# One block-maximum task of each B unit moves from the last group of a slot into the first group of the next slot

## The chip, the cores and the metric

The kernel runs on one core of one Trainium2 chip. The metric is the device time of one execution in microseconds. Engines are called as in the profile: PE is the matrix engine, PEld its weight loads, DVE the vector engine, ACT the scalar engine, POOL the GpSimd engine, SP the queue that issues most DMAs.

## The reference, cut to what matters

Two attentions over the same 2048 tokens (width 512, 32 heads of 16) are mixed by a gate. A is a segmented attention with a compressive memory: four segments of 512 tokens, each with softmax inside the segment. B is an ordinary attention over all 2048 keys:

```
qkv = (x @ wqkv)...;  scores = q k^T * Dh**-0.5;  p = softmax(scores);  o = p v      # B
out = g * (A @ wo_a) + (1 - g) * (B @ wo_b)
```

The softmax needs the maximum of each row of scores before the exponentials. Here that maximum comes from a separate product: the scores are computed twice, once only for their maxima, once transposed for the exponentials.

## The kernel before, in words

After a projection phase (about the first 335 us) the work is 32 units of A and 32 of B; a unit is four heads by 512 queries. They are done in 32 **slots**, loop variable `k`: slot `k` does B unit `32 + k` and then A unit `k`. A slot has 37 **groups**, loop variable `n`: groups 0 to 31 are B's, groups 32 to 36 are A's. The order in which each engine takes instructions is the order in which this code writes them.

A B group is written by `t_group` and `pvs`. `t_group` (line 537) issues two matmuls of 64 rows by 128 keys by 512 queries, here called T0 (rows 0 to 63 of the array) and T1 (rows 64 to 127), into two of the three score banks `tb`, `tb`, `mb`, and ACT takes the exponential of each (line 543). `pvs` issues the product of earlier exponentials with V into the one bank `pvb` (line 559).

Beside its own work, slot `k` computes the maxima of units that come later. The list `plan[k, n]` holds these tasks. A **B task** `s_b` (lines 474 and 476) is two matmuls S (rows 64 to 127, then rows 0 to 63) into one of two buffers `sbk` (two banks each, taken in turn by `rot("s", SBK)`) and one DVE reduction over both banks. Each B unit has 32 of them. For `k >= 1` the tasks of unit `33 + k` are spread one to a group, twelve over groups 20 to 31 of slot `k - 1` and twenty over groups 0 to 19 of slot `k`. In slot 0 some of groups 0 to 19 have two tasks. Six **A tasks** `s_a` (lines 452 to 462) with their reductions follow the T matmuls of A groups 32 to 36.

A B task stands between T0 and T1 of its group (argument `between`), so that S on rows 64 to 127 runs beside T0, and S on rows 0 to 63 beside T1.

At group 0 `pvs` finishes the previous A unit: the last product into `pvb`, then `fin_copy` (line 566), a DVE copy of `pvb` to `pvs`. Group 1 has no V product. From slot 9 on, group 1 is followed by `out_mm` (line 625), twelve matmuls of the output projection. Group 2 starts the next use of `pvb`.

Of the kernel before, what the change touches and what calls it, by code (L numbers as in the profile page):

```python
# [23 lines left out]
NT = SEQ // 128  # L24
# [10 lines left out]
def gated_mix_kernel(ctx, tc, xt, wq, wk, wv, wo, beta, wqkv, wob, gate_w, out):  # L35
# [370 lines left out]
    def load_q(u):  # L406
        kd, qd, c = UN[u]
        load_qk(q_of(u), kd, 0, qd, c)

    def load_ka(u):  # L410
        kd, qd, c = UN[u]
        load_qk(KA[u % 2], kd, 1, qd, c)

    def load_kb(k, c=None):
        dst = KB[k % 3] if c is None else KB[k % 3][:, :, c * C:(c + 1) * C]
        load_qk(dst, "B", 1, k % 8, c)
# [6 lines left out]
    def load_vb(g):  # L423
        v_src(VB[g % 2], "B", g % 4, None)

    def load_va(u):
        kd, qd, c = UN[u]
        v_src(VA[(u // 2) % 2], "A", qd // 2, c)
# [51 lines left out]
    def m_chain(k):  # L480
        mx = pair_max(k)
        if k == 1:
            nc.vector.memset(mx[:, 0], 0.0)
        if k < 32:
            nc.vector.tensor_reduce(mx[:, 1], MXB.pop(32 + k).rearrange("q j p i c -> q (j p) i c"), axis=AX.X,
                                    op=OP.max)
        else:
            nc.vector.memset(mx[:, 1], 0.0)
        del MX[k]
        mx = mx.rearrange("q u h i -> q (u h i)")  # L490
        m8 = M8[k] = W.tile([128, 2, 32], FT, name="m8")
        hi = W.tile([128, 32], FR, name="mhi")
        if 8 <= k < 32:
            nc.gpsimd.tensor_scalar(mx, mx, -1.0, None, op0=OP.mult)
            nc.gpsimd.tensor_copy(hi, mx)
            nc.gpsimd.tensor_copy(m8[:, 0], hi)
            nc.gpsimd.tensor_tensor(m8[:, 1], mx, hi, op=OP.subtract)
        else:
            nc.vector.tensor_scalar(hi, mx, -1.0, None, op0=OP.mult)
            nc.vector.tensor_copy(m8[:, 0], hi)  # L500
            nc.vector.scalar_tensor_tensor(m8[:, 1], mx, -1.0, hi, op0=OP.mult, op1=OP.subtract)
# [20 lines left out]
    def t_group(u, n, banks, between=()):  # L522


        kd, qd, c = UN[u]
        bs = [bank(banks) for _ in range(2)]
        c0 = 0
        for it, hs in (((n // 2, (n % 2 * 2, n % 2 * 2 + 1)),) if kd == "B" else GA[n]):
            q0 = 128 * it if kd == "A" else 0
            w = C - q0  # L530
            pn = it if kd == "B" else it % 2
            for j, h in enumerate(hs):
                if j:
                    for f in between:
                        f()
                r = slice(64 * j, 64 * j + 64)
                nc.tensor.matmul(bs[j][:, c0:c0 + w], k_of(u, h // 2)[r, 128 * it:128 * it + 128],  # L537
                                 q_of(u)[r, h // 2, q0:], start=True, stop=True)
                PT[u, it, h] = PTILE[pn % 2][:, 2 + j if (kd, it) == ("A", 2) else h][:, c0:c0 + w]
            c0 += w  # L540
        for j in range(2):
            pt = PTILE[pn % 2][:, 2 + j if (kd, n) == ("A", 4) else hs[j]]
            nc.scalar.activation(pt, bs[j], AF.Exp, scale=SCALE)  # L543
            if kd == "A":
                m = pt[:, :128] if n < 2 else pt.rearrange("p (a t) -> p a t", a=4)[:, ::3 if n < 4 else 2]
                nc.gpsimd.affine_select(out=m, in_=m, pattern=[[1, 128]] if n < 2 else [[0, 2], [1, 128]],  # L546
                                        compare_op=OP.is_ge, fill=0.0, base=0, channel_multiplier=-1)
# [119 lines left out]
    def todo(fn, *a):  # L667
        return lambda: fn(*a)
# [90 lines left out]
    for blk in range(16):  # L759
# [9 lines left out]
        n = blk + 1 + (c == 2)  # L769
# [74 lines left out]
    def late():  # L844
        proj.close()
        L = AT["L"] = ctx.enter_context(tc.tile_pool(name="late", bufs=1))
        VB[1] = L.tile([128, NT, 8, E + 1], FT, name="vb1")
        AT["o"] = [L.tile([128, 4, 2, C], FT, name=f"o{n}") for n in range(2)]
        AT["wh"] = L.tile([128, 4, 2, DM], FR, name="wh")
        AT["wl"] = L.tile([128, 4, 2, DM], FR, name="wl")  # L850
        AT["d"] = [L.tile([128, C], FT, name=f"d{n}") for n in range(2)]
        AT["oh"] = L.tile([128, 4, 2, 128], FR, name="oh")
        AT["ol"] = L.tile([128, 4, 2, 128], FR, name="ol")
        for p in range(2):
            set_aux(KB[2][:, p], 0)
# [6 lines left out]
    def pvs(k, n):  # L862

        ua, ub = k, 32 + k
        if n == 0:
            if k:
                pv(ua - 1, 2)
                fin_copy(ua - 1)
        elif k == 31 and n < 2 * NT:
            if n % 2 and n > 1:  # L870
                pv(ub, n // 2 - 1)
        elif 2 <= n < 2 * NT + 2:
            pv(ub, n // 2 - 1, n % 2 * 256, n % 2 * 256 + 256)
            if n == 2 * NT + 1:
                fin_copy(ub)
        elif n > 2 * NT + 1:
            m = n - 2 * NT - 2
            if m < 2:
                pv(ua, 0, 256 * m, 256 * m + 256)
            else:  # L880
                pv(ua, 1)
                pv(ua, 3)
# [13 lines left out]
    def beside(k, it):  # L896

        for f, it0, u in ((fin_load, NT + 1, 32 + k), (fin_rec, 5, 31 + k), (fin_bc, 6, 31 + k),
                          (fin_load, 1, k - 1), (fin_rec, 6, k - 1), (fin_bc, S_LAST + 2, k - 1)):
            if it == it0 and (k or it0 > NT):  # L900
                f(u)
        c, j = divmod(k - 1, 8)
        if k and j % 2:
            for kd, it0 in (("B", 9), ("A", 13)):
                if it == it0:
                    fin_norm(kd, j // 2, c)
        if k >= 8 and k % 2 == 0 and it == NT + 2:
            out_split(k // 8 - 1, k // 2 % 4)
        if (k, it) == (31, 4):
            grest = AT["grest"] = AT["o"][0][64:, 0, 0]  # L910
            nc.sync.dma_start(grest, GD[3 * C:].rearrange("(o t) -> o t", o=1).to_broadcast([64, C]))
        if (k, it) == (31, 9):
            grest = AT["grest"]
            nc.vector.tensor_scalar(grest, grest, nh[64:, 3:4], None, op0=OP.mult)
        if (k, it) == (31, NT + 2):
            fin_rec(63)
        if k == 31 and it == 13:
            o = AT["o"][1][:64, 3, 0]
            nc.gpsimd.tensor_tensor(o, o, AT["d"][0][:64], op=OP.mult)
        if k == 31 and it < 8 and it % 2 == 0:  # L920
            for a in range(2):
                tail_split(it // 2, slice(0, 3), a)
# [3 lines left out]
    plan = {}  # L926
# [5 lines left out]
    for k in range(31):  # L932
# [5 lines left out]
        for n, t in enumerate(ST_A):  # L938
            plan.setdefault((k, 2 * NT + n - (n > 2)), []).append(todo(s_a, k + 1, *t))

    for k in range(32):
        ua, ub = k, 32 + k
        banks = T3 + [b[:, 0] for b in SBK] * (k == 31)
        for n in range(NG):
            it = n // 2 if n < NG - 1 else NT + 2
            mid = plan.pop((k, n)) if n < 2 * NT and (k, n) in plan else []
            t_group(*(ub, n) if n < 2 * NT else (ua, n - 2 * NT), banks, mid)
            for f in plan.get((k, n), []) + ex[k][0].get(n, []):
                f()
            pvs(k, n)  # L950
            for f in ex[k][1].get(n, []):
                f()
            if n % 2 == 0 and n < NG - 1:
                continue
            beside(k, it)
            if it == S_LAST:
                m_chain(k + 1)
            if it == 4 and not k:
                late()
            if it == 4 and not k:  # L960
                load_q(ub + 2)
                for c in range(NC4):
                    load_kb(2, c)
            if it == NT and k < 29:
                load_q(ub + 3)
                load_kb(k + 3)
            if it == 6 and k < 31:
                load_q(ua + 1)
                load_ka(ua + 1)
                if (ua + 1) % 2 == 0:  # L970
                    load_va(ua + 1)
            if it == 9:
                if k % 2 == 0 and k < 30:
                    load_vb(k // 2 + 1)
                if 1 <= k <= 4:
                    load_wo(k - 1)
# [55 lines left out]
```

## Time and profile before

| what | value |
|---|---|
| time, median of 3 runs | 1946.82 us (1943.4 to 2188.65) |
| profiled execution, its own time | 1946.74 us |
| its span, first to last instruction | 1945.0 us |
| mean granted PE clock | 0.997 |
| busy share of the span | PE 99%, DVE 83%, ACT 74%, POOL 15% |

The span is what the trace covers; the profiled execution's own time is 1.74 us more and lies 0.08 us from the median. A row of the timeline has the start, the length, the engine, the line, the operation with its output and inputs, and in square brackets the idle time of that engine just before with what ended it. Rows that follow each other with the same form are merged (x2, x8).

### The profile page before, as it was taken

To read this page: it belongs to the slowest core of one execution; us is meant where nothing else is said; L and a number is where in the kernel's file an instruction comes from. 1 tells how busy PE (TensorE), PEld (TensorE's weight loads), DVE (VectorE), ACT (ScalarE), POOL (GpSimd) and SP (SyncE) were. 2 spreads that over 40 slices of the span, in tenths; PEclk is the share of its full clock that TensorE was granted. 3 is DMA by queue.
4 is the path that set the end of the run, shared out by engine and by line. 5 is a ranking of instruction groups with operands and counts; after the bars stand their busy time and mean duration, and the time that the engine had idled before them with its cause. 6 is when DMAs were issued, how large, how long until landed. Compare 5 with 4: busy or idle time off the path is not lost.

```text
span 1945.0 us, 43560 instructions
## 1 busy us (share of the span) xinstructions
PE 1922.5 (99%) x17485; PEld 931.0 (48%) x17485; DVE 1622.1 (83%) x1726; ACT 1434.8 (74%) x2699; POOL 298.4 (15%) x593
## 2 busy tenths in 40 slices
PE   7999999999999999999999999999999999999999
PEld 5887777444344444444444444444444444444445
DVE  6135766899999999999999999999999999999942
ACT  4233333688888888888888888888888888888884
POOL 5200000011111111111111111111111111111022
PEclk9999999999999999999999999999999999999999
DMA  7666656745444444443445454544444443434111
GB/s 217 163 207 185 196 193 173 176 96 116 98 117 88 105 87 105 87 116 87 116 87 114 87 115 87 116 88 108 94 97 107 96 105 87 104 87 110 50 48 58
DMA packets 163790, 222.49 MB, mean 114 GB/s; under 512 B 39916, under 2 KB 90556, under 8 KB 157828
## 3 DMA queue, kind: packets, MB, share of 16 engines
q1 hardware_dynamic: 159284, 211.41, 44.1%
q0 software_dynamic: 3248, 8.03, 2.3%
q8 instruction: 138, 2.26, 0.5%
q14 instruction: 64, 0.52, 0.1%
q10 hardware_dynamic: 1056, 0.26, 0.1%
HBM read 147.95 MB, written 68.16 MB: 111 GB/s over the span
## 4 chain that ended last, share of the span: by engine, by line
PE 96%; DVE 2%; DMA 1%; SPq 1%; issue 0%; ACT 0%; DVEq 0%; ACTq 0%
PE pvb L559 33%; PE tb L537 18%; PE sbk L474 12%; PE mb L537 9%; PE tb L304 5%; PE sbk L452 3%; PE tb L625 2%; PE mb L304 2%; PE sbk L287 1%; PE tb L287 1%; PE mb L625 1%; PE pvb L304 1%; PE sbk L456 1%; PE mb L287 1%; PE pvb L287 1%; PE tb L652 1%
## 5 line engine op out<-in xcount | busy, mean ns | idle before, releaser
L476 DVE TENSOR_REDUCE mxb<-sbk 128x2 f32<-128x1024 f32 x1024 | 1225.8, 1223 | 61.0 <-PE tb L537 30.6
L543 ACT ACTIVATE raw<-tb 128x512 f32<-128x512 f32 x1555 | 887.6, 598 | 148.2 <-PE tb L537 103.6
L559 PE MATMUL pvb<-raw,vb 128*17 128x256 f32 (+1 forms) x8072 | 639.9, 388 | 0.0
L543 ACT ACTIVATE raw<-mb 128x512 f32<-128x512 f32 x782 | 467.6, 598 | 72.3 <-PE mb L537 45.7
L474 PE MATMUL sbk<-xh,qb 64*128 64x512 f32 x1344 | 477.6, 444 | 3.5 <-DVE mxb L476 2.1
L537 PE MATMUL tb<-qb,xh 64*128 64x512 f32 x872 | 353.3, 443 | 0.0
L559 PEld LDWEIGHTS pvb<-raw,vb 128*17 128x17 f32 x8072 | 135.0, 95 | 341.3 <-issue 335.9
L474 PE MATMUL sbk<-kb,qb 64*128 64x512 f32 x704 | 240.9, 444 | 0.0
L537 PEld LDWEIGHTS tb<-qb,xh 64*128 64x128 f32 x872 | 146.4, 184 | 176.6 <-issue 90.1
L537 PE MATMUL mb<-qb,xh 64*128 64x512 f32 x445 | 199.0, 447 | 0.0
L474 PEld LDWEIGHTS sbk<-xh,qb 64*128 64x128 f32 x1344 | 190.6, 184 | 8.7 <-DVE mxb L476 6.3
L537 PE MATMUL tb<-qb,kb 64*128 64x512 f32 x470 | 191.0, 446 | 0.9 <-DVE st L314 0.9
L546 POOL TENSOR_SCALAR_AFFINE_SELECT raw<-raw 128x256 f32<-128x256 f32 (+1 forms) x320 | 115.6, 361 | 357.7 <-ACT raw L543 349.9
L460 DVE TENSOR_REDUCE mx<-sbk 128x2 f32<-128x768 f32 (+1 forms) x128 | 136.7, 1090 | 23.7 <-PE sbk L456 20.9
L537 PEld LDWEIGHTS mb<-qb,xh 64*128 64x128 f32 x445 | 82.0, 184 | 94.9 <-issue 50.6
L537 PEld LDWEIGHTS tb<-qb,kb 64*128 64x128 f32 x470 | 79.2, 184 | 99.0 <-issue 53.1
L599 POOL TENSOR_TENSOR o<-o,d 128x512 f32<-128x512 f32 x31 | 39.7, 1280 | 477.7 <-DMA d<-rd 388.5
L537 PE MATMUL mb<-qb,kb 64*128 64x512 f32 x234 | 104.1, 445 | 0.0
L474 PEld LDWEIGHTS sbk<-kb,qb 64*128 64x128 f32 x704 | 96.1, 184 | 5.2 <-issue 3.4
L559 PE MATMUL pvb<-raw,va 128*17 128x256 f32 (+2 forms) x1280 | 94.7, 384 | 0.8 <-ACT pvs L568 0.8
L452 PE MATMUL sbk<-ka,qa 64*128 64x256 f32 (+3 forms) x512 | 88.0, 358 | 1.1
L311 ACT ACTIVATE st<-tb 128x512 fp32r<-128x512 f32 x33 | 19.8, 599 | 81.1 <-DVE phi L310 46.8
(288 smaller groups left out, 1864.3 us busy)
## 6 DMA issues: line engine op xcount, KB each, us to landing
xh<-dB SPq DMA_DIRECT2D x38, 512.0 KB
vb<-vdB SPq DMA_DIRECT2D x16, 1088.0 KB
dB<-st SPq DMA_DIRECT2D x64, 256.0 KB
dA<-st SPq DMA_DIRECT2D x64, 256.0 KB
pd<-pvs SPq DMA_DIRECT2D x64, 256.0 KB
kb<-dB SPq DMA_DIRECT2D x22, 512.0 KB
xh<-dB SPq DMA_DIRECT2D x38, 256.0 KB
qb<-dB SPq DMA_DIRECT2D x64, 128.0 KB
```

The source lines that it names most:

```text
L287: nc.tensor.matmul(b, lhs, WV[wi][:, k, :], start=n == 0, stop=n == 11)
L304: nc.tensor.matmul(b, WS[ws][w][wi][:, k, :], (XH, XL)[xi][c][:, k, :], start=n == 0, stop=n == 11)
L452: nc.tensor.matmul(b[:, j, c0:c0 + n], q_of(u)[r, p, i * 128:(i + 1) * 128], k_of(u, p)[r, :n], start=True, stop=False)
L460: nc.vector.tensor_reduce(m[:, :, p, i], b[:, :, :n], axis=AX.X, op=OP.max)
L474: nc.tensor.matmul(b[:, j], q_of(u)[r, p, i * 128:(i + 1) * 128], k_of(u, p)[r, kc * C:(kc + 1) * C], start=True, stop=True)
L476: nc.vector.tensor_reduce(MXB[u][:, :, p, i, kc], b, axis=AX.X, op=OP.max)
L537: nc.tensor.matmul(bs[j][:, c0:c0 + w], k_of(u, h // 2)[r, 128 * it:128 * it + 128], q_of(u)[r, h // 2, q0:], start=True, stop=True)
L543: nc.scalar.activation(pt, bs[j], AF.Exp, scale=SCALE)
L546: nc.gpsimd.affine_select(out=m, in_=m, pattern=[[1, 128]] if n < 2 else [[0, 2], [1, 128]], compare_op=OP.is_ge, fill=0.0, base=0, channe ...
L559: nc.tensor.matmul(PVB[32 * h:32 * h + E + 1, q0 + lo:q0 + hi], vt[:, it, 4 * q + h, :], pt[:, lo:hi], start=it == 0 and lo == 0, stop=it ...
L599: nc.gpsimd.tensor_tensor(o, o, d, op=OP.mult)
L625: nc.tensor.matmul(b, (AT["oh"], AT["ol"])[oi][:, g, a], (AT["wh"], AT["wl"])[wi][:, g, a], start=n == 0, stop=n == 11)
```

## The change

For `k` from 0 to 29 the task of group 31 of slot `k` is appended to the list of group 0 of slot `k + 1`, which so holds two. Of each list only the last task is put between T0 and T1; the others are issued after `t_group`.

```
+    for k in range(30):
+        plan[k + 1, 0] += plan.pop((k, 2 * NT - 1))
     for k in range(32):
...
-            mid = plan.pop((k, n)) if n < 2 * NT and (k, n) in plan else []
+            mid = [plan[k, n].pop()] if n < 2 * NT and (k, n) in plan else []
             t_group(*(ub, n) if n < 2 * NT else (ua, n - 2 * NT), banks, mid)
             for f in plan.get((k, n), []) + ex[k][0].get(n, []):
                 f()
```

The first place is PE at the end of slot 0, group 31 and the T matmuls of group 32 (`qb`, `kb`, `xh`: queries and keys of B; `qa`, `ka`: of A; one piece of the difference).

```order
 L559 MATMUL pvb<-raw_86,vb_75 17x256 x4
 L537 MATMUL mb<-qb_70,kb_89 128x512
-L474 MATMUL sbk_115<-xh_88,qb_69 128x512 x2
 L537 MATMUL tb_111<-qb_70,kb_89 128x512
 L559 MATMUL pvb<-raw_86,vb_75 17x256 x4
 L537 MATMUL tb_110<-qa_73,ka_71 128x512
 L537 MATMUL mb<-qa_73,ka_71 128x512
```

T0 and T1 of group 31 now stand next to each other, with no S between them.

The second place is PE at groups 0, 1 and 2 of slot 1, before:

```order
L537 MATMUL mb<-qb_68,xh_87 128x512
L474 MATMUL sbk_114<-xh_88,qb_69 128x512 x2
L537 MATMUL tb_111<-qb_68,xh_87 128x512
L559 MATMUL pvb<-raw_86,va_76 17x256 x4
L537 MATMUL tb_110<-qb_68,xh_87 128x512
L474 MATMUL sbk_115<-xh_88,qb_69 128x512 x2
L537 MATMUL mb<-qb_68,xh_87 128x512
```

and with the change:

```order
L537 MATMUL mb<-qb_68,xh_87 128x512
L474 MATMUL sbk_115<-xh_88,qb_69 128x512 x2
L537 MATMUL tb_111<-qb_68,xh_87 128x512
L474 MATMUL sbk_114<-xh_88,qb_69 128x512 x2
L559 MATMUL pvb<-raw_86,va_76 17x256 x4
L537 MATMUL tb_110<-qb_68,xh_87 128x512
L474 MATMUL sbk_115<-xh_88,qb_69 128x512 x2
L537 MATMUL mb<-qb_68,xh_87 128x512
```

The moved task stands between T0 and T1 of group 0 and writes `sbk_115`; the task that stood there follows after T1 into `sbk_114`; the task of group 1 writes `sbk_115` again, one group after the moved one.

The third place is DVE at the same boundary, from the last B reductions of the slot over the six A reductions, before:

```order
L476 TENSOR_REDUCE mxb<-sbk_114 128x2
L476 TENSOR_REDUCE mxb<-sbk_115 128x2
L460 TENSOR_REDUCE mx<-sbk_114 128x2
L460 TENSOR_REDUCE mx<-sbk_115 128x2
L460 TENSOR_REDUCE mx<-sbk_114 128x2
L460 TENSOR_REDUCE mx<-sbk_115 128x2
L462 TENSOR_REDUCE mx<-sbk_114 128x4
L462 TENSOR_REDUCE mx<-sbk_115 128x4
L476 TENSOR_REDUCE mxb<-sbk_114 128x2
L566 COPY pvs<-pvb 128x512
L476 TENSOR_REDUCE mxb<-sbk_115 128x2
```

and with the change:

```order
L476 TENSOR_REDUCE mxb<-sbk_114 128x2
L460 TENSOR_REDUCE mx<-sbk_115 128x2
L460 TENSOR_REDUCE mx<-sbk_114 128x2
L460 TENSOR_REDUCE mx<-sbk_115 128x2
L460 TENSOR_REDUCE mx<-sbk_114 128x2
L462 TENSOR_REDUCE mx<-sbk_115 128x4
L462 TENSOR_REDUCE mx<-sbk_114 128x4
L476 TENSOR_REDUCE mxb<-sbk_115 128x2
L476 TENSOR_REDUCE mxb<-sbk_114 128x2
L566 COPY pvs<-pvb 128x512
L476 TENSOR_REDUCE mxb<-sbk_115 128x2
```

One reduction has left the place ahead of the A reductions, and two now stand ahead of the copy of `pvb`.

In slot 0 the six groups that have two tasks change too: both pairs S stood between T0 and T1, now the second pair follows T1. The number of instructions on every engine is the same.

More of the change, by code (lines that the diff above doesn't have):

```diff
@@ L939, in gated_mix_kernel @@
             plan.setdefault((k, 2 * NT + n - (n > 2)), []).append(todo(s_a, k + 1, *t))
+    for k in range(30):
+        plan[k + 1, 0] += plan.pop((k, 2 * NT - 1))
     for k in range(32):
@@ L945, in gated_mix_kernel @@
             it = n // 2 if n < NG - 1 else NT + 2
-            mid = plan.pop((k, n)) if n < 2 * NT and (k, n) in plan else []
+            mid = [plan[k, n].pop()] if n < 2 * NT and (k, n) in plan else []
             t_group(*(ub, n) if n < 2 * NT else (ua, n - 2 * NT), banks, mid)
```

## The prediction

> **What bounds the kernel now.** I read the page first (busy shares, the chain that ended last), then the table of windows for whole slots, then the timeline around the place where one slot ends and the next begins.
>
> ```profile
> PE 1922.5 (99%) x17485; PEld 931.0 (48%) x17485; DVE 1622.1 (83%) x1726; ACT 1434.8 (74%) x2699; POOL 298.4 (15%) x593
> PE 96%; DVE 2%; DMA 1%; SPq 1%; issue 0%; ACT 0%; DVEq 0%; ACTq 0%
> 450.86:498.33 47.47, 47.43 (x496) 19.17 (x492) 45.70 (x47) 40.76 (x76) 9.91 (x17) 1.00 0.53 121
> 1032.02:1081.60 49.58, 49.54 (x508) 20.82 (x504) 46.46 (x45) 40.85 (x77) 8.35 (x17) 1.00 0.49 114
> ```
>
> The chain is PE for 96%. The window rows (slice: length, then busy time of PE, PEld, DVE, ACT, POOL, clock, DMA share) are one early and one late slot: PE is busy from end to end at full clock, DVE for 45.70 of 47.47 us and 46.46 of 49.58 us. So PE sets the pace and DVE is close behind it; whatever makes PE wait for DVE, or adds to PE's order, is on the path. The 49.58 us slot is longer because it has `out_mm`.
>
> Late slot, its start (I call the first T0 of a slot time T; here 1032.02):
>
> ```profile
> 1023.01 0.50 PE L537 MATMUL tb<-qb,xh 64*128 64x512 f32 x1
> ...
> 1032.02 0.50 PE L537 MATMUL tb<-qb,xh 64*128 64x512 f32 x1
> 1032.03 0.73 PE L474 MATMUL sbk<-kb,qb 64*128 64x512 f32 x2
> 1032.36 0.39 PE L537 MATMUL mb<-qb,xh 64*128 64x512 f32 x1
> 1032.69 0.63 PE L559 MATMUL pvb<-raw,va 128*17 128x256 f32 x8
> 1032.79 1.23 DVE L476 TENSOR_REDUCE mxb<-sbk 128x2 f32<-128x1024 f32 x1 [0.95 <-PE mb L537]
> 1033.24 0.50 PE L537 MATMUL tb<-qb,xh 64*128 64x512 f32 x1
> 1033.25 0.73 PE L474 MATMUL sbk<-kb,qb 64*128 64x512 f32 x2
> 1033.58 0.39 PE L537 MATMUL tb<-qb,xh 64*128 64x512 f32 x1
> 1033.91 1.19 PE L625 MATMUL mb<-wh,oh 128*128 128x512 f32 x4
> ...
> 1036.87 0.50 PE L537 MATMUL tb<-qb,xh 64*128 64x512 f32 x1
> 1036.97 0.69 DVE L632 TENSOR_TENSOR yo<-mb,yo 128x512 f32<-128x512 f32 x1 [1.23 <-PE mb L625]
> 1037.63 12.18 DVE L476 TENSOR_REDUCE mxb<-sbk 128x2 f32<-128x1024 f32 x10
> ```
>
> The first row is T0 of group 31 of the slot before. T0 and S of group 0 start together (1032.02 and 1032.03), T1 0.34 later beside the second S: four matmuls in two rounds of about 0.33 us. The V product follows at T + 0.67 and the next group at T + 1.22. The reduction starts at T + 0.77. `out_mm` starts at 1033.91 and group 2 at 1036.87; DVE then has caught up (1.23 us idle).
>
> Early slot, no `out_mm` (T = 498.33):
>
> ```profile
> 498.33 0.49 PE L537 MATMUL mb<-qb,kb 64*128 64x512 f32 x1
> 499.10 1.23 DVE L476 TENSOR_REDUCE mxb<-sbk 128x2 f32<-128x1024 f32 x1 [0.94 <-PE tb L537]
> 500.24 0.68 DVE L566 COPY pvs<-pvb 128x512 f32<-128x512 f32 x1
> 500.38 0.19 PEld L474 LDWEIGHTS sbk<-xh,qb 64*128 64x128 f32 x2 [0.19 <-DVE mxb L476]
> 500.84 6.92 DVE L476 TENSOR_REDUCE mxb<-sbk 128x2 f32<-128x1024 f32 x6
> 501.22 0.18 PEld L559 LDWEIGHTS pvb<-raw,vb 128*17 128x17 f32 x8 [0.24 <-DVE pvs L566]
> 501.82 0.18 PEld L537 LDWEIGHTS mb<-qb,kb 64*128 64x128 f32 x1 [0.42 <-issue]
> 502.11 0.19 PEld L474 LDWEIGHTS sbk<-xh,qb 64*128 64x128 f32 x2
> 503.33 0.18 PEld L537 LDWEIGHTS tb<-qb,kb 64*128 64x128 f32 x1 [0.42 <-ACT raw L543]
> ```
>
> This gives the price of a DVE wait. The S of group 2 (500.38) waits for the reduction of group 0, which started at 499.10 in the same buffer: 1.28 us from a reduction's start to the next S there. The S of group 3 (502.11) comes 1.27 us after the reduction of group 1 (500.84). The V product of group 2 (501.22) waits for the copy, 0.98 us after its start (500.24). On DVE the copy starts 1.14 us after a reduction, the next reduction 0.60 us after the copy, and reductions in a row come every 1.14 us (6.92 us for six, 1.23 for the last, so 5.69 for five).
>
> **The change part by part.** *Group 31 loses a pair S.* PE's two rounds become one, 0.33 us less, if nothing else holds group 32.
>
> ```profile
> 489.28 0.49 PE L537 MATMUL mb<-qb,xh 64*128 64x512 f32 x1
> 489.87 0.60 ACT L543 ACTIVATE raw<-mb 128x512 f32<-128x512 f32 x1 [0.19 <-PE mb L537]
> 490.52 0.50 PE L537 MATMUL mb<-qa,ka 64*128 64x512 f32 x1
> 490.86 0.49 PE L452 MATMUL sbk<-ka,qa 64*128 64x512 f32 x2
> 491.47 1.23 DVE L460 TENSOR_REDUCE mx<-sbk 128x2 f32<-128x1024 f32 x1 [0.19 <-PE sbk L456]
> ```
>
> T0 of group 31 (489.28) goes into `mb`; ACT reads it from 489.87 to 490.47; T1 of group 32 writes `mb` again at 490.52, 0.05 us after ACT is done. T0 of group 31 does not move, so neither does that exponential, nor T1 of group 32, nor the A task behind it on PE (490.86), nor its reduction (491.47), before which DVE was idle. I take a gain of nothing. The bounds are a gain of 0.33 us a slot (30 slots: 9.9 us) and a loss of 0.10 us (3 us), if the weight load for `mb`, now also waiting, shows its length.
>
> *Group 0 has a second pair S, then group 1.* The pair costs one round: T0 beside S, S beside T1, S beside S, V product at T + 1.01, group 1 at T + 1.56. That is not what decides. The S of group 1 needs the buffer of the moved task, whose reduction starts at T + 0.77 as now; so it comes at T + 0.77 + 1.28 = T + 2.05. Before it came at T + 1.23 (1033.25 - 1032.02). PE, which takes its instructions in order, is 0.82 us late. Of this 0.34 is the pair and 0.48 waiting; had the pair cost two rounds, the S would come no later.
>
> *Slots 9 to 30* (22 of the 30): `out_mm` follows, 0.82 us late. DVE does the second reduction from T + 1.91, the copy from T + 3.05 and the reduction of group 1 from T + 3.65 to 4.9; group 2 starts at T + 4.85 + 0.82 = 5.67. DVE has caught up there as before. 22 x 0.82 = 18.0 us.
>
> *Slots 1 to 8*: no such cover. The S of group 2 needs the second reduction: T + 1.91 + 1.28 = 3.19. The V product of group 2 waits for the copy: T + 3.05 + 0.98 = 4.03; group 3 begins 0.60 us later (501.82 after 501.22) at 4.63; its S needs the reduction of group 1: T + 3.65 + 1.27 = 4.92. Before it came at 502.11 - 498.33 = 3.78. Late by 1.14 us, one reduction; from there PE and DVE stand to each other as before. 8 x 1.14 = 9.1 us.
>
> By the Trainium skill, VectorE: DVE Perf Modes, section "The DRAIN you can't avoid", the next vector operation does not start until the pipe of the one before has emptied, except where nothing holds it. By the rule reductions would follow each other at their full 1.23 us and not at 1.14, and the early slots would cost 8 x 1.23 = 9.8 us, 0.7 us more. The trace shows the exception: six of 1.23 us fit into 6.92 us.
>
> *The copy and its DMA* come 1.14 to 2 us later. Behind the copy's store wait the loads for the reciprocals; in the late slot the copy starts at 1033.93 and the reciprocals come some 15 us later:
>
> ```profile
> 1033.93 0.68 DVE L566 COPY pvs<-pvb 128x512 f32<-128x512 f32 x1
> 1049.73 0.24 DVE L583 RECIPROCAL rec<-rec 128x16 f32<-128x16 f32 x1
> ```
>
> Covered, cost nothing; without that cover it would be up to 2 us a slot.
>
> *Slot 0*, six groups with two tasks:
>
> ```profile
> 344.61 0.50 PE L474 MATMUL sbk<-xh,qb 64*128 64x512 f32 x2 [0.41 <-DVE mxb L476]
> 344.94 0.39 PE L537 MATMUL tb<-qb,kb 64*128 64x512 f32 x1
> ```
>
> The second pair waits for a buffer, and T1 stood behind it. Now T1 runs before the wait and the pair takes one round after it and not two: a gain of 0.33 where there was a wait. Between 0 and 6 x 0.33 = 2 us; I take 1 us.
>
> Sum: 18.0 + 9.1 - 1 = 26.1 us. The profiled execution took 1946.74 us, and 1946.7 + 26.1 is 1973 us. That execution lies 0.08 us from the median, so the same holds for the median.
>
> **The rivals.** *The end of the slot does give the 0.33 us back*: ACT's chain is not what holds group 32. For it: PE shows no idle time there; against it: T1 of group 32 comes 0.05 us after the exponential. 1973 - 9.9 = 1963 us.
>
> *Not slower.* The stretch from group 31 to the next slot is paced by DVE's queue, and the reduction that no longer stands ahead of the six A reductions lets all of them come earlier. It pays from the point where this stretch shrinks by the 0.82 us (late) or 1.14 us (early) lost behind group 0. If it shrinks by a whole reduction, 30 x 1.14 = 34.2 us stand against 27.1; with slot 0 that is 8 us gained, 1939 us. Against it: DVE is idle 0.19 us before the first A reduction and 0.95 us before the first of the slot; it waits for PE there and not the other way.
>
> *The delay comes back.* DVE does not catch up behind `out_mm` or group 3, and the small operations between the reductions, which now find it a whole reduction late, make PE wait again. The two reciprocal steps cost DVE about 0.4 us each (a reciprocal of 0.24 us and a product); 0.8 us in 30 slots is 24 us more, 1997 us. It decides from the point where a reduction starts over 0.39 us late (a buffer is needed again after 2.44 us, and 0.77 + 1.28 of it are used). Against it: the ten reductions at 1037.63 take 12.18 us, 1.22 each, which is PE's pace, so DVE has no backlog behind `out_mm`.
>
> *Nothing changes*: the moved pair only swaps places and PE hides the buffer wait, because weights can be loaded meanwhile. 1947 us. Against it: at 500.38 it is the weight load itself that waits.
>
> **How the numbers follow.** Forecast 0.70; the 0.33 us given back 0.13; not slower 0.04; the delay comes back 0.09; nothing changes 0.04. The range goes from 1960 us (the gain at group 31 and slot 0 at its best, 1962, less 2 us for the spread of the runs) to 1986 us (loss at group 31 of 3 us, slot 0 giving nothing, and a third of the returning delay). A measurement of this kernel can tell about 2% from no change, 39 us, so 1908 to 1986 counts as the same. Over that lies only the returning delay, 0.08; under it next to nothing, 0.01; within, 0.91.
>
> **What would show it.** Right: slots 1 to 8 last about 48.6 us instead of 47.4, slots 9 to 30 about 50.4 instead of 49.6; in group 1 a new wait of S for the DVE reduction, about 0.5 us, 30 times; DVE idle about 1.3 us at the end of a slot, where one reduction went; T1 of group 32 still 0.05 us after ACT; the copy 1.1 to 1.2 us later after T. Wrong: the stretch from the first T0 of group 31 to the next slot's (now 1023.01 to 1032.02 in the late slot, 9.0 us) shrinks by 0.3 us or more, or PE waits for reductions between groups 12 and 20.

## The result and the profile after

The median of four runs is 1972.28 us (1968.01 to 1973.22), against 1947.03 us before. The ratio is 1.0135 with a 95% interval of [1.0124, 1.0147]: 26 us slower (24 to 29), clear of the spread but under 2%. The ratio is of fast runs alone, so the one of 2188.65 us before is not in it. The profiled execution has a span of 1970.8 us, 25.8 us more.

The page of after, busy shares and the chain by engine:

```profile
PE 1939.9 (98%) x17485; PEld 938.0 (48%) x17485; DVE 1621.3 (82%) x1726; ACT 1435.4 (73%) x2699; POOL 297.5 (15%) x593
PE 94%; DVE 4%; issue 1%; DMA 1%; ACT 0%; SPq 0%; DVEq 0%; ACTq 0%
```

The work is the same (DVE 1621.3 us against 1622.1). DVE's share of the chain doubled from 2% to 4%. Of the 25.8 us lost, 17.4 stand in PE's own busy time (1939.9 against 1922.5), so the loss cannot be read from PE's idle time. It is seen in the list of waits (engine, tile, line, what it waited for: us in total, times, longest), here the same entry before and after:

```profile
PEld sbk L474 <- DVE mxb L476: 7.1, 17, 1.4
PEld sbk L474 <- DVE mxb L476: 27.4, 54, 1.3
```

The start of a late slot (T = 1043.79), chosen rows. The first L474 row is the moved task's pair S, the second one the pair that stood there before:

```profile
1043.79 0.50 PE L537 MATMUL tb<-qb,xh 64*128 64x512 f32 x1
1043.79 0.72 PE L474 MATMUL sbk<-kb,qb 64*128 64x512 f32 x2
1044.13 0.39 PE L537 MATMUL mb<-qb,xh 64*128 64x512 f32 x1
1044.36 0.39 PE L474 MATMUL sbk<-kb,qb 64*128 64x512 f32 x2
1044.55 2.36 DVE L476 TENSOR_REDUCE mxb<-sbk 128x2 f32<-128x1024 f32 x2 [0.94 <-PE mb L537]
1044.68 0.63 PE L559 MATMUL pvb<-raw,va 128*17 128x256 f32 x8
1045.24 0.50 PE L537 MATMUL tb<-qb,xh 64*128 64x512 f32 x1
1045.83 0.19 PEld L474 LDWEIGHTS sbk<-kb,qb 64*128 64x128 f32 x2 [0.41 <-DVE mxb L476]
1046.17 0.39 PE L537 MATMUL tb<-qb,xh 64*128 64x512 f32 x1
1046.49 1.20 PE L625 MATMUL mb<-wh,oh 128*128 128x512 f32 x4
1046.82 0.68 DVE L566 COPY pvs<-pvb 128x512 f32<-128x512 f32 x1
```

The second pair S goes in one round; the V product starts at T + 0.89, before the pair's last matmul has ended. T0 of group 1 starts at T + 1.45. Its S stands until T + 2.04, 1.28 us after the reduction of the moved task began, and `out_mm` starts at T + 2.70 instead of T + 1.89: 0.81 us late. T0 of group 1 runs alone for 0.50 us of that wait, which counts as PE's busy time. The start of the slot is paced by DVE, though PE is the busy engine.

The start of an early slot (T = 499.27), chosen weight loads: T0 of group 1, S of group 1, S of group 2, V product of group 2, S of group 3, T0 of group 4:

```profile
500.71 0.18 PEld L537 LDWEIGHTS tb<-qb,kb 64*128 64x128 f32 x1 [0.42 <-issue]
501.31 0.19 PEld L474 LDWEIGHTS sbk<-xh,qb 64*128 64x128 f32 x2 [0.42 <-DVE mxb L476]
502.44 0.19 PEld L474 LDWEIGHTS sbk<-xh,qb 64*128 64x128 f32 x2 [0.83 <-DVE mxb L476]
503.10 0.13 PEld L559 LDWEIGHTS pvb<-raw,vb 128*17 128x17 f32 x8 [0.36 <-DVE pvs L566]
504.18 0.18 PEld L474 LDWEIGHTS sbk<-xh,qb 64*128 64x128 f32 x2 [0.33 <-DVE mxb L476]
505.38 0.18 PEld L537 LDWEIGHTS tb<-qb,kb 64*128 64x128 f32 x1 [0.42 <-issue]
```

Three waits for reductions follow each other, at the S of groups 1, 2 and 3, with the V product's wait for the copy between them, and group 4 starts at T + 6.11 instead of T + 5.00.

The end of a late slot: T0 and T1 of group 31, ACT's exponential of T0, the two T of group 32, the A task and its reduction:

```profile
1034.78 0.50 PE L537 MATMUL tb<-qb,xh 64*128 64x512 f32 x1
1034.79 0.49 PE L537 MATMUL mb<-qb,xh 64*128 64x512 f32 x1
1035.38 0.60 ACT L543 ACTIVATE raw<-tb 128x512 f32<-128x512 f32 x1 [0.20 <-PE tb L537]
1035.77 0.76 PE L537 MATMUL tb<-qa,ka 64*128 64x512 f32 x2
1036.37 0.46 PE L452 MATMUL sbk<-ka,qa 64*128 64x512 f32 x2
1037.01 4.35 DVE L460 TENSOR_REDUCE mx<-sbk 128x2 f32<-128x1024 f32 x4 [1.46 <-PE sbk L456]
```

PE is indeed done with group 31 earlier and starts group 32 at 1035.77, 0.99 us after group 31 and no longer 1.22. But the pair of T now takes 0.76 us together instead of 0.52: its second one waits for ACT (1035.38 + 0.60). The A task comes at 1036.37, 1.59 us after T0 of group 31, as before (1024.59 after 1023.01 was 1.58). From T0 of group 31 to the next slot it is 1043.79 - 1034.78 = 9.01 us, before 1032.02 - 1023.01 = 9.01. DVE, with one reduction less ahead of the A reductions, is idle 1.46 us before them, where it was 0.24.

The length of a slot, from the first L462 reduction to that of the next slots in each trace (early: mean of slots 5 and 6, late: mean of seven slots from about 1030 us on):

| kernel | early slot, us | late slot, us |
|---|---|---|
| before | 47.46 | 49.59 |
| after | 48.58 | 50.40 |
| late_only | 47.46 | 50.38 |
| early_only | 48.60 | 49.59 |
| no_second | 47.74 | 50.41 |
| half_reduce | 48.05 | 49.87 |
| half_exp | 48.40 | 50.19 |
| drop31 | 47.44 | 49.58 |
| early36 | 47.86 | 49.56 |
| slot0_only | 47.44 | 49.58 |

### The profile page after: what moved, and what is told of

The parts are those of the page before. It is cut to its first block, busy times and chain, and to the rows that moved or that the text cites. A ratio compares the mean times of both kernels' runs of the same rounds, so it can differ in the third digit from the quotient of the medians.

```text
span 1970.8 us, 43560 instructions
## 1 busy us (share of the span) xinstructions
PE 1939.9 (98%) x17485; PEld 938.0 (48%) x17485; DVE 1621.3 (82%) x1726; ACT 1435.4 (73%) x2699; POOL 297.5 (15%) x593
## 4 chain that ended last, share of the span: by engine, by line
PE 94%; DVE 4%; issue 1%; DMA 1%; ACT 0%; SPq 0%; DVEq 0%; ACTq 0%
PE pvb L559 32%; PE tb L537 17%; PE sbk L474 12%; PE mb L537 9%; PE tb L304 5%; PE sbk L452 3%; DVE mxb L476 3%; PE tb L625 2%; PE mb L304 2%; PE sbk L287 1%; PE tb L287 1%; PE pvb L304 1%; PE mb L625 1%; PE sbk L456 1%; PE mb L287 1%; PE pvb L287 1%
## 5 line engine op out<-in xcount | busy, mean ns | idle before, releaser
L474 PE MATMUL sbk<-xh,qb 64*128 64x512 f32 x1344 | 463.5, 445 | 8.2 <-DVE mxb L476 3.4
L474 PE MATMUL sbk<-kb,qb 64*128 64x512 f32 x704 | 233.7, 444 | 3.1 <-DVE mxb L476 2.1
L474 PEld LDWEIGHTS sbk<-xh,qb 64*128 64x128 f32 x1344 | 186.6, 185 | 22.6 <-DVE mxb L476 18.4
L474 PEld LDWEIGHTS sbk<-kb,qb 64*128 64x128 f32 x704 | 94.0, 185 | 13.6 <-DVE mxb L476 9.0
L537 PE MATMUL tb<-qa,ka 64*128 64x512 f32 (+3 forms) x339 | 81.1, 372 | 0.0
```

What stands on the lines that cost most here:

```text
L474: nc.tensor.matmul(b[:, j], q_of(u)[r, p, i * 128:(i + 1) * 128], k_of(u, p)[r, kc * C:(kc + 1) * C], start=True, stop=True)
```

## The experiments

The theory on trial: the loss is the wait of group 1's S for the reduction of the moved task (*buffer theory*), the second pair's own round on PE is hidden in that wait, and leaving group 31 gains nothing since ACT holds group 32. The rivals: the loss is PE's own time for the pair; the delay comes back later in the slot; DVE's backlog at the end of a slot counts. Ratios below are to the kernel before (medians 1944.83 and 1945.08 us in the two sets), with 95% intervals; 0.1% is 1.9 us. Times in the expectations count from about 1947 us, so it is the differences that are to be compared.

**Only the late slots, only the early ones.**

```
-    for k in range(30):
+    for k in range(8, 30):        # late_only;  range(8): early_only
         plan[k + 1, 0] += plan.pop((k, 2 * NT - 1))
...
-    mid = [plan[k, n].pop()] if ...
+    mid = ([plan[k, n].pop()] if k else plan.pop((k, n))) if ...
```

> The task is moved only into slots 9 to 30, which have the output projection behind group 1; slot 0 is as before. By the buffer theory each of the 22 slots loses 0.82 us (the S of group 1 waits for the moved task's reduction): 18.0 us over the kernel before, about 1965. By the rival that only the pair's own round of 0.34 us is lost: 7.5 us, about 1954.5. By the rival that the delay comes back between groups 12 and 20: 22 x 1.6, 35 us, about 1982.

Measured 1963.18 us, 1.0097 [1.0083, 1.0111], 18.9 us (16 to 22). The table has 22 x 0.79 = 17.4 us in the late slots (added up over all 22 of them it is 18.0) and nothing in the early ones. The buffer theory's 18.0 fits; the pair's own 7.5 us and the returning delay's 35 us are both out.

> The task is moved only into slots 1 to 8, which have no output projection behind group 1; slot 0 is as before. By the buffer theory 8 x 1.14 = 9.1 us, about 1956. By the rival that an early slot costs no more than a late one: 8 x 0.82 = 6.6 us, 1953.6.

Measured 1953.80 us, 1.0039 [1.0027, 1.0051], 7.6 us (5 to 10). The time holds both answers; the trace tells them apart: an early slot is 1.14 us longer (48.60 against 47.46), not 0.82.

**The second task of group 0 left out.** A small memset stands in for it, and its turn of the buffer is kept.

```
+    def s_skip(u, i, p, kc):
+        rot("s", SBK)
+        nc.vector.memset(MXB[u][:, :, p, i, kc], 0.0)
...
+        plan[k + 1, 0] = [todo(s_skip, u, *ts[12])] + plan.pop((k, 2 * NT - 1))
```

> As the change, but the second task of group 0 in slots 1 to 30 is left out: its pair S and its reduction are not done, a small DVE memset stands in for it (so these maxima are not computed), and its turn of the buffer is kept. PE has one round less and DVE one reduction less in each slot. By the buffer theory the S of group 1 still waits for the reduction of the moved task, T + 2.05, so the late slots lose the same 0.82 us (18.0 in all), the early ones 0.31 us (2.5), slot 0 gains 0.8: about 1967. By the rival that the pair's own PE time is lost beside the wait, 0.34 us a slot comes back at least: 22 x 0.48 = 10.6, about 1957.

Measured 1963.76 us, 1.0098 [1.0085, 1.0111], 19.1 us (17 to 22). One round of PE and one reduction less in 30 slots, and the late slots are as long as with the change (50.41 against 50.40); the early ones keep 0.28 us (0.31 was expected). Late slot, T = 1033.91; first the reduction of the moved task, T0 of group 1, then its S:

```profile
1034.68 1.23 DVE L476 TENSOR_REDUCE mxb<-sbk 128x2 f32<-128x1024 f32 x1 [0.95 <-PE mb L541]
1035.13 0.50 PE L541 MATMUL tb<-qb,xh 64*128 64x512 f32 x1
1035.85 0.06 DVE L480 MEMSET mxb<- 128x2 f32 x1
1035.96 0.19 PEld L474 LDWEIGHTS sbk<-kb,qb 64*128 64x128 f32 x2 [0.65 <-DVE mxb L480]
```

T0 of group 1 comes at T + 1.22, and S still at T + 2.05. The row names the memset because it ends with the reduction (both at 1035.91); only the reduction reads that buffer. This is the run that tells the theories apart: with the wait in place the pair's own round costs a late slot nothing.

**The moved task's reduction made short.** It reads 256 of 512 columns of each bank.

```
+        nc.vector.tensor_reduce(MXB[u][:, :, p, i, kc], b[:, :, :256], axis=AX.X, op=OP.max)   # moved task only
```

> As the change, but the reduction of the moved task reads only the first 256 of the 512 columns of each bank (so these maxima are partial); its matmuls and all others stay. The reduction should take about 0.69 us instead of 1.23, so that the S of group 1 may come at T + 1.5, before PE gets there (T + 1.56). By the buffer theory the wait goes and the pair's round is left: late slots lose 0.33 us (7.3), early ones 0.61 (4.9), slot 0 gains 0.8: about 1958.5. By the rival that the loss is PE's order and not the reduction's length: 1972 as the change.

Measured 1955.06 us, 1.0063 [1.0042, 1.0084], 12.3 us (8 to 16), about half of the change's loss. The late slots are 0.28 us longer than before (0.33 expected), the early ones 0.59 (0.61). Late slot, T = 1035.84; the short reduction, T0 of group 1, its S:

```profile
1036.61 0.69 DVE L484 TENSOR_REDUCE mxb<-sbk 128x2 f32<-128x512 f32 x1 [0.94 <-PE mb L545]
1037.29 0.50 PE L545 MATMUL tb<-qb,xh 64*128 64x512 f32 x1
1037.35 0.23 PEld L474 LDWEIGHTS sbk<-kb,qb 64*128 64x128 f32 x2
```

The S of group 1 stands 0.06 us behind T0 instead of 0.6 (0.01 in the kernel before). The wait is all but gone, and what is left is the pair's own round: T0 of group 1 comes at T + 1.45 instead of T + 1.22, 0.23 us, and with the 0.05 us that are left of the wait that makes the 0.28.

**Group 31's exponential made short**, the first tile over 256 of 512 columns.

```
+            e = slice(0, 256) if kd == "B" and n == 2 * NT - 1 and j == 0 and u < 62 else slice(0, C)
-            nc.scalar.activation(pt, bs[j], AF.Exp, scale=SCALE)
+            nc.scalar.activation(pt[:, e], bs[j][:, e], AF.Exp, scale=SCALE)
```

> As the change, but in slots 0 to 29 the exponential of the first score tile of group 31 (T0) covers 256 of 512 columns (so its other half is stale). That exponential should take about 0.39 us instead of 0.60, the bank comes free 0.21 us earlier. By the theory that ACT's exponential holds T1 of group 32, the stretch from T0 of group 31 to the next slot shrinks from 9.01 to about 8.80 us and the time by 30 x 0.21 = 6.3 us, to about 1966. By the rival that something else holds group 32: 1972 and 9.01 us.

Measured 1964.31 us, 1.0095 [1.0082, 1.0108] against the change's 1.0135: some 8 us less (6.3 was expected). A late slot is 0.21 us shorter than with the change and an early one 0.18, which makes 6.1 us in 30 slots. T0 of group 31, its exponential and the T pair of group 32:

```profile
1032.46 0.50 PE L537 MATMUL tb<-qb,xh 64*128 64x512 f32 x1
1033.06 0.38 ACT L544 ACTIVATE raw<-tb 128x256 f32<-128x256 f32 x1 [0.20 <-PE mb L537]
1033.45 0.54 PE L537 MATMUL tb<-qa,ka 64*128 64x512 f32 x2
```

The exponential is 0.22 us shorter and the T pair of group 32 takes 0.54 us instead of 0.76. The stretch from T0 of group 31 to the next slot is 8.81 us (8.80 was expected) and no longer 9.01. What ACT gives up at group 31, the slot gains: ACT does hold group 32.

**Group 31's task left out of the kernel before** (a memset in its place, so 30 pairs and 30 reductions less).

```
+        plan[k, 2 * NT - 1] = [todo(s_skip, u, *ts[11])]
```

> The kernel before, with the task of group 31 of slots 0 to 29 left out altogether (a small DVE memset instead, so these maxima are not computed). One pair S and one reduction less in each of 30 slots. By the theory that the place at group 31 costs PE nothing: the stretch from T0 of group 31 to the next slot stays 9.01 us and the time 1946 to 1947. By the rival that the pair holds PE there: 30 x 0.33 = 9.9 us less, 1937. By the rival that its reduction delays the six A reductions: up to 30 x 1.14 = 34 us less, 1913.

Measured 1945.48 us, 1.0006 [0.9997, 1.0016]. Nothing is gained, on PE or on DVE; slots are 47.44 and 49.58 us, and the stretch from T0 of group 31 to the next slot is 9.02 us. The task was free where it stood.

**Slot 0's order alone.**

```
-            mid = plan.pop((k, n)) if n < 2 * NT and (k, n) in plan else []
+            mid = [plan[k, n].pop()] if n < 2 * NT and (k, n) in plan else []
```

> No task is moved to another group; only the second task of slot 0's double groups goes behind T1. From the two traces the part of slot 0 that is not the lower clock at 345 us was 0.8 us: 1946 against 1947, hardly measurable; the stretch from the first reduction of slot 0 at about 330 us to the first one of slot 1 is 72 us (before, 74.3, with 1.6 us of lower clock in it; after, 72.0). By the rival that the order alone gains the whole 2.3 us there, the stretch in a run of the kernel before without a lower clock would also be 74.3, and the time 1944.6.

Measured 1942.56 us, 0.9990 [0.9980, 0.9999], 1.9 us less (0.2 to 3.9), the only version that beat the kernel before, and barely. The time alone holds both answers, 0.8 us and 2.3. From the L341 row in slot 0 (a DVE row at about 331 us) to the first L462 row behind it, in traces without the lower clock described below, it is 67.9 us with the old order (drop31, the only such trace) and 67.1 to 67.8 with the new one (half_exp, after, early36, slot0_only, no_second): 0.2 to 0.9 us. So by the traces most of the 2.3 us between the first two is not the order's.

**A version that might have been faster.** In slots 1 to 8 group 1's task goes behind the A tasks of the slot before, and ACT does the copy:

```
+    for k in range(8):
+        plan[k, 2 * NT + 4] += plan.pop((k + 1, 1))
...
-        if u < 31:
+        if 8 <= u < 31:                # fin_copy: DVE; else ACT
```

> A version that may beat the kernel before: slots 9 to 30 as before; in slots 1 to 8, where groups 2 and 3 wait for DVE, the task of group 1 goes into group 36 of the slot before, behind the A tasks, where DVE is idle 0.95 us, and the copy of the bank of the V products is done by ACT; slot 0 with the second task behind T1. From the rows: group 4 starts about 0.5 us earlier after T0 in each of 8 slots, with slot 0 some 4.8 us in all, 1942. If the exponentials, which now wait behind ACT's copy, hold the T matmuls of group 2 instead: 1946 to 1950.

Measured 1948.40 us, 1.0013 [1.0003, 1.0023], slower by 2.5 us (0.6 to 4.5). T0 of group 0 is at 496.78 in this slot; the first T of group 2, its second one, and the first T of group 4:

```profile
498.45 0.18 PEld L537 LDWEIGHTS tb<-qb,kb 64*128 64x128 f32 x1 [0.27 <-ACT raw L543]
499.43 0.18 PEld L537 LDWEIGHTS tb<-qb,kb 64*128 64x128 f32 x1 [0.68 <-ACT raw L543]
501.67 0.18 PEld L537 LDWEIGHTS tb<-qb,kb 64*128 64x128 f32 x1 [0.42 <-ACT raw L543]
```

No wait for DVE is left, but ACT, with the copy in its queue, holds group 2, and group 4 starts at T + 4.89 instead of T + 5.00. That 0.11 us does not pay for the pair S behind the A tasks, whose cost the expectation had left out: from T0 of group 31 to the next slot it is now 9.5 us in these eight slots instead of 9.0. The early slot is 0.40 us longer.

## Why the prediction was right, point by point

*Group 31 gains nothing*: right. The stretch is 9.01 us before and after; half_exp shows what holds it, drop31 that the reduction there held nothing either.

*Group 1's S at T + 2.05, 0.82 us late, the pair itself not deciding*: right, T + 2.04 and 0.81 (the pair took 0.23 us of PE and not 0.34, so PE came to group 1 at T + 1.45 and not 1.56, which the wait swallowed); shown by no_second and half_reduce. From slot 9 to the end the trace of after is 18.1 us longer (25.8 less 7.67, the shift of slot 9's first reduction, 784.99 to 792.66); 18.0 was predicted.

*Early slots 1.14 us*: right, 1.12 by the table (48.58 against 47.46). One step inside was off: the V product of group 2 follows the copy's start by less than the 0.98 us taken from the trace of before (there T1 of group 2 had started only at 500.80 and stood ahead of it); it started at T + 3.83 and not at 4.03. That cost the sum nothing, for group 3's S waits for the reduction anyway, at T + 4.91 (4.92 predicted). From slot 1 to slot 9 the two traces part by 10.2 us: 8 x 1.12 = 9.0, and the rest is one more slow vector operation (last section).

*Slot 0, 1 us*: the direction was right and the size rather too large, 0.2 to 0.9 us. The two traces part by 2.3 us there. The bookkeeping by the L341 row (331.61 before, 331.40 after) and the first reductions of slots 1 and 9 (404.19 and 784.99 before, 401.65 and 792.66 after): -0.2 ahead of that row, -2.3 to slot 1, +10.2, +18.1, together 25.8. But 1.5 of the 2.3 us are a lower clock in the trace of before. That the spans differ by almost exactly the 26.1 us forecast is therefore in part luck: the one slow vector operation more (+1.2) and the lower clock (-1.5) happen to cancel. The 18.0 and 9.1 us stand by the slots themselves.

*The copy is late and hidden*: right. It starts at T + 3.03 instead of T + 1.91.

*The rivals.* The 0.33 us did not come back at group 31; DVE's backlog did not count; the delay did not return after group 3, since late_only and the table leave no room for it; and the wait was not hidden.

*The vector engine's drain.* Reductions in a row still overlap (two of 1.23 us in 2.36 us), as in the trace of before, and an early slot lost 1.12 us, not 1.23.

## What to carry to other kernels

Before moving work off a busy stretch, ask what ends that stretch: here PE was 99% busy, and yet the task in group 31 was free, because the exponential of another engine held the next group. With two buffers in turn, a second task in one group can cost not its own time but what the cycle of the buffer asks for, if that is longer: from the consumer's start to the next producer it is 1.28 us here, while PE comes round in 0.68 us (the 1.45 us of group 0 with the pair, less 0.77 us until the reduction starts), which leaves a stall of 0.6 us. A pair of rows in which a wait of this kind already occurs, like the early slots here, is the best price list for a wait that the change will add.

## What the runs showed of the hardware

**A vector operation that waited for GpSimd.** In slot 1 of after the last step of the maxima's split took 1.28 us, and in slot 2 its usual 0.18; beside the first stands a GpSimd operation:

```profile
430.36 1.31 POOL L612 TENSOR_TENSOR wl<-o,wh 128x512 fp32r<-128x512 f32 x1
430.44 1.28 DVE L501 SCALAR_TENSOR_TENSOR m<-mx,mhi 128x32 f32<-128x32 f32 x1
480.12 0.18 DVE L501 SCALAR_TENSOR_TENSOR m<-mx,mhi 128x32 f32<-128x32 f32 x1
```

The GpSimd operation ends at 431.67, the vector one at 431.72. It happened in slots 1 and 3 of after and in slot 3 of before, where the two started 0.08 us apart too, and PE waited 1.2 to 1.4 us each time. It stands in slot 3 of half_reduce, half_exp, drop31 and slot0_only too, so the change does not decide it; the GpSimd operations start when a DMA lands (the one before this, at 429.67, had waited 28.40 us for it), and the two meet or do not. The Trainium skill, SBUF — State Buffer, section "Who interferes with whom", says that a vector operation with two SBUF inputs contends with a GpSimd operation that reads SBUF, and that the contention is an exclusive lock; these rows agree. Not only operations with two inputs are slowed: in late_only the COPY just ahead (L500, one input, 0.18 us in slot 1 of after) took 1.29 us beside the same GpSimd operation. It was not tried by itself.

**A short stretch of lower clock.** In the trace of before, busy times and clock (the column after POOL) of one projection job in slot 0 and the next one like it:

```profile
345.27:349.81 4.54, 4.54 (x13) 3.31 (x12) 1.55 (x2) 0.60 (x1) 0.62 (x1) 0.62 0.70 231
353.09:356.07 2.98, 2.98 (x13) 2.17 (x12) 1.63 (x2) 0.60 (x1) 0.00 (x0) 1.00 1.03 87
```

The same twelve matmuls took 1.56 us longer at a granted clock of 0.62. Between 342 and 348 us this stands in the traces of before, late_only, early_only and half_reduce (0.72 to 0.79 over those 6 us) and not in those of after, no_second, half_exp, drop31, slot0_only and early36 (1.00). Its cause is open. A difference of 2 us between two single traces of this kernel means nothing without a look at it.
